# A weight's third part made by TensorE and ScalarE instead of VectorE, in a linear attention and gated FFN kernel

## The chip, the cores and the metric

The kernel runs on one core of one Trainium2 chip. The metric is the device time of one launch in microseconds, median of several runs. TensorE appears in the profile as PE (matmuls) and PEld (weight loads), VectorE as DVE, ScalarE as ACT, GpSimd as POOL, SyncE as SP. The kernel's transfers are issued by SyncE (SPq) and, fewer, by GpSimd (POOLq).

## What is computed

Two stages, in float32. The first is a recurrence with a decay per channel, over 768 steps, for 4 batches of 8 heads of 48 channels:

```
state = alpha[t][:, None] * state + outer(k[t], v[t])
y[t]  = q[t] @ state
```

The second takes y, laid out as x of 3072 tokens by 384, through a multiplicative FFN: `a = x @ w1; b = x @ w2; out = ((a * b) @ w3) @ w_out`, with w1 and w2 of 384x1024, w3 of 1024x1024 and w_out of 1024x384. The four weights arrive as 64-bit floats and must be turned into 32-bit ones on the chip.

## The kernel before

**The recurrence** is done in 24 chunks of 128 steps, six for each batch. For chunk n: `logs` takes the logarithm of alpha on ScalarE, `decays` sums it along time by a matmul with a triangle of ones (L271, and L274 from chunk 10) and takes two exponentials on ScalarE (L277, L278), `decayed` multiplies k and q by them on VectorE (L287), `transposed` turns them on TensorE and ScalarE copies them out of PSUM (L309, L311), `scores` multiplies q and k on TensorE and VectorE masks the product (L349, L352), `outer` forms the chunk's own state on TensorE (L321), and `attend_state` and `attend` add up y on TensorE (L369, L375), which ScalarE copies out (L379). The copies go to DRAM (xd, L246) and come back transposed three chunks at a time (xT, L391).

**The FFN's matmuls** run in fp32r, a float32 type that TensorE multiplies with a shortened mantissa. To reach float32's precision every operand is split in three parts h, l and m, and a product is made of h·h, l·l and m·m: `products` (L405) runs over the parts, and its callers weigh the sums. For w1 and w2, h is the value rounded and divided by P = 4096, l is what is left (w - P·h), and m is (P + 1)·h - w, which is h - l.

**Conversion.** `load_gates` fetches one unit of w1 or w2, 128x512 values as 64-bit words (raw, L189), and turns them into float32 by ScalarE (L197, L202) and VectorE (L198, L201, L204, L205, L207); then h by ScalarE (L214), l by VectorE (L216) and m by VectorE (L217). There are twelve units. The first six (half 0) hold the first 512 columns of both weights and are needed by the first gates; the other six (half 1) come later. `convert` advances these generators by a step at a time from the chunk loop.

**Order.** The loop over n (from line 583 on) calls, for each n: store, the loads of later chunks, attend_state(n - 1), scores(n), transposed(n + 1), a step of conversion, advance(n), attend(n - 1), outer(n), a piece of gate work, conversion, decayed(n + 2), logs(n + 4), decays(n + 3), conversion, gate work. From chunk 4 on x of three chunks is loaded (xT), split in its three parts by `split_x` (L397 on ScalarE, L398 and L399 on VectorE), and `gate` pieces (L405, L414, L416) fill TensorE between the chunks' own matmuls; the first such piece runs in chunk 7. A scheduler sets the order in which the instructions stand on each engine; every engine then works strictly in that order, and semaphores hold an instruction until its inputs are there and its buffer is free. PSUM is a ring of eight banks (`bank()`), taken in turn by all stages: eight in a chunk without gate work. Loads have three buffers for alpha and for k and q, five for v and four for raw words. After the chunks comes the rest of the gates, the folding of w3 and w_out into one, and the projection, almost all of it L405 on TensorE.

Of the kernel before, what the change touches and what calls it, by code (L numbers as in the profile page):

```python
# [10 lines left out]
FP32 = mybir.dt.float32  # L11
FP32R = mybir.dt.float32r
# [4 lines left out]
ALU = mybir.AluOpType  # L17
# [3 lines left out]
P = 4096.0  # L21
# [27 lines left out]
def kernel(  # L49
# [12 lines left out]
    nc = tc.nc  # L62
    B, H, S, D = q.shape
    C = 128
# [4 lines left out]
    NP = H // 2  # L69
# [12 lines left out]
    def pool(name, bufs, stack=ctx, **kw):  # L82
        return stack.enter_context(tc.tile_pool(name=name, bufs=bufs, **kw))
# [15 lines left out]
    p1 = pool("p1", 1, stack=part1, side="right", reuse_waits="tile")  # L99
    inp = pool("inp", 3, stack=part1, side="right", reuse_waits="tile")  # L100
    work = pool("work", 2, stack=part1, side="right", reuse_waits="tile")

    def bank():
        return ps.tile([C, 512], FP32, tag="bank", name="bank")
# [24 lines left out]
    def load_a(n):  # L129
        if n < N:  # L130
            st["a", n] = inp.tile([C, H, D], FP32, tag="ac", name="ac")
            nc.sync.dma_start(out=st["a", n], in_=rows(alpha, n))
# [8 lines left out]
    def load_v(n):  # L141
        if n < N:
            st["v", n] = vs[n % len(vs)]
            nc.sync.dma_start(out=st["v", n][:, :, 0:D], in_=rows(v, n))
# [10 lines left out]
    ident = const.tile([C, C], FP32, name="ident")  # L155
# [1 line left out]

    w12 = [p.tile([C, 3, 2, KM, CW], FP32R, name=f"w12{i}") for i, p in enumerate((w12ap, const))]

    utri = p1.tile([C, C], FP32, name="utri")  # L160
    after = p1.tile([C, C], FP32, name="after")

    sums = p1.tile([C, 2, C], FP32R, name="sums")
    keep = p1.tile([C, C], I32, name="keep")
    qks = [p1.tile([C, 2, H, DP], FP32, name=f"qk{i}") for i in range(3)]
    Ts = [p1.tile([C, NP, DP], FP32, name=f"T{i}") for i in range(2)]
# [11 lines left out]
    for x in qks:  # L178
        nc.vector.memset(x[:, :, :, D:], 0.0)
    make_identity(nc, ident)  # L180
    for x in Ts + decs:
        nc.gpsimd.memset(x, 0.0)

    def to_fp32(dst, *srcs):

        n, m = len(srcs) * srcs[0].shape[1], srcs[0].shape[1]
        raw = rawp.tile([C, n], I64, tag="raw", name="raw")
        for i, src in enumerate(srcs):
            nc.sync.dma_start(out=raw[:, ds(i * m, m)], in_=src)  # L189
        yield  # L190
        words = raw.bitcast(U32).rearrange("p (n w) -> p n w", w=2)
        low, high = words[:, :, 0], words[:, :, 1]

        mant = cvt.tile([C, n], FP32, tag="mant", name="mant")
        top = mant.bitcast(U32)
        rest = cvt.tile([C, n], FP32, tag="rest", name="rest", bufs=2)
        nc.scalar.activation(rest, low, AF.Copy, scale=2.0 ** -52)  # L197
        nc.vector.tensor_scalar(top, high, 0x000FFFFF, 0x00100000, op0=ALU.bitwise_and, op1=ALU.bitwise_or)  # L198

        power = cvt.tile([C, n], U32, tag="power", name="power", bufs=2)  # L200
        nc.vector.tensor_scalar(power, high, 20, 0x7FF, op0=ALU.logical_shift_right, op1=ALU.bitwise_and)  # L201
        nc.scalar.activation(power, power, AF.Relu, scale=2.0 ** 23, bias=rebias)  # L202
        yield
        nc.vector.scalar_tensor_tensor(mant, top, 2.0 ** -20, rest, op0=ALU.mult, op1=ALU.add)  # L204
        nc.vector.scalar_tensor_tensor(power, high, 0x80000000, power, op0=ALU.bitwise_and, op1=ALU.bitwise_or)  # L205
        to = mant if dst is None else dst()
        nc.vector.tensor_mul(to, mant, power.bitcast(FP32))  # L207
        yield
        return to

    def load_gates(i, kk, half):
        w = yield from to_fp32(None, (moe_w1, moe_w2)[i][ds(kk * C, C), ds(half * CW, CW)])
        h, l, m = (w12[half][:, x, i, kk, :] for x in range(3))
        nc.scalar.activation(h, w, AF.Copy, scale=(1.0 - 2.0 ** -13) / P)  # L214
        yield
        nc.vector.scalar_tensor_tensor(l, h.bitcast(FP32), -P, w, op0=ALU.mult, op1=ALU.add)  # L216
        nc.vector.scalar_tensor_tensor(m, h.bitcast(FP32), P + 1.0, w, op0=ALU.mult, op1=ALU.subtract)  # L217

    weights, begun = deque(), deque()

    def fetch(ahead=3):
        while weights and len(begun) < ahead:
# [19 lines left out]
    def store():  # L242

        while later:
            dst, src = later.popleft()
            nc.sync.dma_start(out=dst, in_=src)  # L246

    def last(n):
        return n % NCH == NCH - 1
# [15 lines left out]
    def decays(n):  # L265
        if n >= N:
            return
        lc = bank()[:, 0:DM]
        la = st.pop(("la", n))
        if n < LATE:  # L270
            nc.tensor.matmul(lc, utri if n % 2 else after, la, start=True, stop=True)  # L271
        else:
            for i in range(2):
                nc.tensor.matmul(lc, sums[:, n % 2], la[:, i], start=(i == 0), stop=(i == 1))  # L274

        e = st["e", n] = work.tile([C, 2, DM], FP32, tag="e", name="e", bufs=3)
        nc.scalar.activation(e[:, 0], lc, AF.Exp, scale=-1.0)  # L277
        mark["e", n] = nc.scalar.activation(e[:, 1], lc, AF.Exp).ins  # L278
        if n in ends:
            nc.gpsimd.dma_start(out=ends[n][0:1], in_=e[0:1, 0])  # L280
        if n + 1 in ends:
            nc.gpsimd.dma_start(out=ends[n + 1][1:2], in_=e[C - 1:C, 1])
        load_ends(n)
# [6 lines left out]
    def load_ends(n):  # L290
        if n not in ends:
            return
        with nc.allow_non_contiguous_dma(reason="single values to partitions"):
            for i in range(2):
                nc.gpsimd.dma_start(out=decs[n // 2 % 2][ds(DP * i, D)].rearrange("d m j -> d (m j)"),
                                    in_=ends[n].rearrange("m (j i d) -> i d (m j)", i=2, d=D)[i])
# [17 lines left out]
    def outer(n):  # L314
        if n >= N or last(n):
            return
        qk, vc = qks[n % 3], st["v", n]
        s1 = bank()[:, 0:NP * D].rearrange("p (j d) -> p j d", j=NP)
        for j in range(NP):
            for i in range(2):  # L320
                nc.tensor.matmul(s1[ds(DP * i, DP), j, :], qk[:, 0, 2 * j + i, :], vc[:, 2 * j + i, 0:D],  # L321
                                 start=True, stop=True)

        if n % 2:
            to = st["T", n] = work.tile([C, NP, D], FP32, tag="tmp", name="tmp")
        else:
            to = Ts[1][:, :, 0:D]
        if n % NCH == 0:
            nc.vector.tensor_copy(out=to, in_=s1)
        else:  # L330
            nc.vector.tensor_add(to, s1, Ts[n % 2][:, :, 0:D])
# [142 lines left out]
    def gate(g, f):  # L474
        yield from (late_gate if late else early_gate)(g, f)
# [73 lines left out]
    def run(pieces):  # L549

        for _ in range(pieces):
            if not fill:
                return
            try:
                next(fill[0])
            except StopIteration:
                fill.popleft()
# [5 lines left out]

    logs(0)
    decays(0)
    decayed(0)
    transposed(0)
# [15 lines left out]
    for n in range(N + 1):  # L583
        store()
        load_v(n + AHEAD - 1)
        load_a(n + 5)
        load_kq(n + AHEAD)
        if n:
            attend_state(n - 1)
        if n < N:  # L590
            scores(n)
        transposed(n + 1)
        if n - 2 in begin:
            g, tiles = begin[n - 2]
            split_x(g, 0)
            fill.extend(gate(g, f) for f in tiles)
        pieces = (0, 3, 3, 2)[(n - 6) % 4] if n > 5 else 0
        if n == 0:
            with after_marks(("qkT", 0)):
                logs(2)  # L600
            decays(2)
            with after_marks(("e", 2)):
                logs(3)
        early = n < 7
        behind = after_marks(("qkT", n + 1), ("qk", n + 1)) if early else ExitStack()
        if n < N - 2:
            with behind:
                convert(2 if n == 0 else 1, 2 if n == 0 else 3)
        advance(n)
        if n:  # L610
            attend(n - 1)
        outer(n)
        run(pieces > 0)
        if early:
            with after_marks(("qkT", n + 1), ("qk", n + 1)):
                convert(1)
        with after_marks(*[("ms", n)] * (n < 3)):
            decayed(n + 2)
        logs(n + 4)
        if n in begin:  # L620
            load_x(begin[n][0])
        convert(early and n > 2)
        run(pieces > 1)
        decays(n + 3)
        if n < N - 2:
            convert(early or n % 3 == 0)
        run(pieces > 2)
        if n == N - 3:
            while begun:
                convert(1)  # L630
            weights.extend(load_out(j) for j in range(KF))
            fetch(4)
# [91 lines left out]
```

## Time and profile before

| | us |
|---|---|
| median of five runs | 482.36 |
| the five runs | 484.13, 483.38, 482.36, 479.44, 479.32 |
| the profiled execution, its time | 484.13 |
| its span, first to last instruction | 482.4 |
| PE busy | 453.9 (94%) |
| DVE busy | 360.0 (75%) |
| ACT busy | 278.9 (58%) |
| POOL busy | 73.7 (15%) |
| mean granted clock of TensorE | 0.989 |

A span is counted from the first instruction's start to the last one's end; the execution's own time is 1.7 us longer. Busy times are averages over stages that are bound by different things, so the stage that a change touches must be looked at by itself. In the chain of waits every piece is the thing that the next piece waited for; "issue" is time for which the profile shows no wait. A transfer's issue is short, its landing some us later.

### The profile page before, as it was taken

To read this page: it belongs to the slowest core of one execution; us is meant where nothing else is said; L and a number is where in the kernel's file an instruction comes from. 1 tells how busy PE (TensorE), PEld (TensorE's weight loads), DVE (VectorE), ACT (ScalarE), POOL (GpSimd) and SP (SyncE) were. 2 spreads that over 40 slices of the span, in tenths; PEclk is the share of its full clock that TensorE was granted. 3 is DMA by queue.
4 is the path that set the end of the run, shared out by engine and by line. 5 is a ranking of instruction groups with operands and counts; after the bars stand their busy time and mean duration, and the time that the engine had idled before them with its cause. 6 is when DMAs were issued, how large, how long until landed. Compare 5 with 4: busy or idle time off the path is not lost.

```text
span 482.4 us, 9968 instructions
## 1 busy us (share of the span) xinstructions
PE 453.9 (94%) x3824; PEld 431.2 (89%) x3824; DVE 360.0 (75%) x582; ACT 278.9 (58%) x550; POOL 73.7 (15%) x138
## 2 busy tenths in 40 slices
PE   4788689999899999999999999999999999999996
PEld 2566479898798998999999999999999999999996
DVE  2779999986979666999999788846541966667761
ACT  4666667766667543899787576645553533333330
POOL 2221132112201300112232111111101100000000
PEclk9889999999899999999999999999999999999999
DMA  9999999899899974557775452122104865555511
GB/s 170 179 187 223 245 194 196 203 205 228 176 220 225 182 252 116 160 179 228 237 228 182 126 179 83 50 100 82 50 34 122 248 204 171 171 171 177 178 50 49
DMA packets 153583, 80.29 MB, mean 166 GB/s; under 512 B 104480, under 2 KB 145568, under 8 KB 153536
## 3 DMA queue, kind: packets, MB, share of 16 engines
q1 hardware_dynamic: 148016, 65.22, 55.4%
q0 software_dynamic: 5520, 14.43, 9.3%
q8 instruction: 30, 0.49, 0.4%
q14 instruction: 17, 0.14, 0.1%
HBM read 57.58 MB, written 22.06 MB: 165 GB/s over the span
## 4 chain that ended last, share of the span: by engine, by line
PE 81%; DVE 7%; DMA 5%; ACT 4%; issue 1%; SPq 1%; DVEq 0%; ACTq 0%
PE bank L405 68%; PE bank L375 3%; DMA ac<-in_alpha_dram 3%; PE bank L349 3%; PE bank L309 2%; DMA xd<-x 2%; PE bank L507 1%; DVE qk L287 1%; PE bank L369 1%; DMA raw<-in_moe_w_dram 1%; DVE ms L352 1%; PE bank L271 1%; PE bank L274 1%; PE bank L321 1%; DVE mant L207 1%
## 5 line engine op out<-in xcount | busy, mean ns | idle before, releaser
L405 PE MATMUL bank<-x,w 128*128 128x384 f32 x1152 | 211.4, 338 | 0.6 <-DVE ms L352 0.3
L405 PEld LDWEIGHTS bank<-x,w 128*128 128x128 f32 x1152 | 200.0, 188 | 2.6 <-issue 1.3
L405 PE MATMUL bank<-w3o,ab 128*128 128x384 f32 x576 | 100.2, 336 | 0.0
L405 PEld LDWEIGHTS bank<-w3o,ab 128*128 128x128 f32 x576 | 99.9, 188 | 0.0
L430 ACT ACTIVATE bank<-bank 128x384 f32<-128x384 f32 x98 | 46.8, 477 | 42.7 <-PE bank L405 42.4
L414 ACT ACTIVATE t<-bank 128x384 f32<-128x384 f32 x62 | 30.3, 493 | 59.3 <-PE bank L405 59.0
L480 POOL DMA_DIRECT2D abd<-ab x46 | 27.6, 599 | 132.2 <-DVE ab L466 124.5
L466 DVE TENSOR_TENSOR ab<-bank,r 128x384 f32<-128x384 f32 x45 | 24.9, 554 | 23.1 <-ACT bank L430 18.0
L536 DVE TENSOR_TENSOR ab<-abl,ab 128x1024 fp32r<-128x1024 f32 x24 | 29.4, 1225 | 13.5 <-ACT ab L535 13.5
L535 ACT ACTIVATE ab<-abl 128x1024 fp32r<-128x1024 f32 x24 | 25.5, 1062 | 21.3 <-PE bank L405 18.9
L405 PE MATMUL bank<-wo,w3T 128*128 128x384 f32 x192 | 35.9, 334 | 0.0
L349 PEld LDWEIGHTS bank<-qkT 48*128 48x128 f32 x384 | 25.5, 200 | 10.1 <-ACT qkT L311 3.7
L349 PE MATMUL bank<-qkT 48*128 48x128 f32 x384 | 30.3, 299 | 3.7 <-ACT qkT L311 2.4
L405 PEld LDWEIGHTS bank<-wo,w3T 128*128 128x128 f32 x192 | 33.5, 188 | 0.0
L352 DVE TENSOR_TENSOR ms<-bank,keep 128x512 int32<-128x512 int32 x48 | 31.2, 684 | 3.1 <-PE bank L349 3.1
L311 ACT COPY qkT<-bank 128x512 f32<-128x512 f32 x48 | 26.0, 586 | 12.6 <-PE bank L309 12.5
L416 DVE SCALAR_TENSOR_TENSOR o<-bank,t 128x384 f32<-128x384 f32 x24 | 13.4, 557 | 23.7 <-issue 15.2
L202 ACT ACTIVATE power<-power,rebias 128x512 uint32<-128x512 uint32 (+1 forms) x36 | 25.0, 698 | 9.5 <-DVE power L201 9.2
L197 ACT ACTIVATE rest<-raw 128x512 f32<-128x512 uint32 (+1 forms) x36 | 23.2, 648 | 12.2 <-DMA raw<-in_moe_w_dram 10.3
L287 DVE TENSOR_TENSOR qk<-kq,e 128x768 f32<-128x768 f32 x24 | 22.9, 953 | 10.0 <-ACT e L278 8.9
L537 DVE SCALAR_TENSOR_TENSOR ab<-ab,abl 128x1024 fp32r<-128x1024 f32 x24 | 29.2, 1218 | 0.0
L416 DVE SCALAR_TENSOR_TENSOR r<-bank,t 128x384 f32<-128x384 f32 x38 | 21.1, 554 | 10.6 <-ACT t L414 7.4
(75 smaller groups left out, 570.2 us busy)
## 6 DMA issues: line engine op xcount, KB each, us to landing
raw<-in_moe_w_dram SPq DMA_DIRECT2D x28, 512.0 KB, 5.3
abl<-abd SPq DMA_DIRECT2D x24, 512.0 KB, 4.6
abd<-ab POOLq DMA_DIRECT2D x46, 192.0 KB, 3.1
xT<-xd POOLq DMA_DIRECT2D x9, 576.0 KB, 4.5
ac<-in_alpha_dram SPq DMA_DIRECT2D x24, 192.0 KB, 5.5
kq<-in_k_dram SPq DMA_DIRECT2D x24, 192.0 KB, 5.5
kq<-in_q_dram SPq DMA_DIRECT2D x24, 192.0 KB, 4.4
v<-in_v_dram SPq DMA_DIRECT2D x24, 192.0 KB, 5.1
```

What stands on the lines that cost most here:

```text
L287: mark["qk", n] = nc.vector.tensor_mul(qks[n % 3][:, :, :, 0:D], st.pop(("kq", n)), st.pop(("e", n)).rearrange("p i (h d) -> p i h d", h=H ...
L311: mark["qkT", n] = nc.scalar.copy(qkT[:, :, :, ds(DP * half, DP)], tp[half]).ins
L349: nc.tensor.matmul(sc[i][:, j, :], qkT[r, 0, j, :], qkT[r, 1, j, :], start=True, stop=True)
L352: masked = nc.vector.tensor_tensor(ms[:, i].bitcast(I32), sc[i].bitcast(I32), keep_bc, op=ALU.bitwise_and)
L405: nc.tensor.matmul(p, w[part][i], x[part][i], start=start and part == parts[0] and i == 0, stop=stop and part == parts[-1] and i == n - 1, ...
L414: nc.scalar.activation(t, p1, AF.Copy, scale=(1.0 + 1.0 / P) * scale)
L416: nc.vector.scalar_tensor_tensor(to, p2, scale, t, op0=ALU.mult, op1=ALU.add)
L430: nc.scalar.activation(p, p, AF.Copy, scale=1.0 + 1.0 / P)
L480: (nc.gpsimd if late else nc.sync).dma_start(out=abd[g][:, f, :], in_=ab)
L535: nc.scalar.activation(t[:, 0], ab, AF.Copy, scale=1.0 - 2.0 ** -13)
L536: nc.vector.tensor_sub(t[:, 1], ab, t[:, 0].bitcast(FP32))
L537: nc.vector.scalar_tensor_tensor(t[:, 2], t[:, 0].bitcast(FP32), -1.0 - 1.0 / P, ab, op0=ALU.mult, op1=ALU.add)
```

## The change

For the six units of half 0, m isn't computed by VectorE any more. Two constant matrices are added, `signs`: the identity and the negative identity, in fp32r. `load_gates` puts (m, h, l) on a list, `thirds`. A new function, `third`, called once in each round of the chunk loop right after `outer(n)`, takes one entry, multiplies h by the identity and adds l times the negative identity in one PSUM bank (two matmuls of 512 columns), and ScalarE copies the bank to m. The units of half 1 keep the VectorE instruction.

The two float32 triangles `utri` and `after` lose their own place: they are made in a buffer of the pool from which the masks `ms` come, which has two, and `decays` reads the fp32r copies of them (`sums`) as float32 in the first ten chunks too. Their values are 0, 1 and -1 in either type.

```diff
-    utri = p1.tile([C, C], FP32, name="utri")
-    after = p1.tile([C, C], FP32, name="after")
+    made = work.tile([C, 2, NP, C], FP32, tag="ms", name="ms")
+    utri, after = made[:, 0, 0, :], made[:, 0, 1, :]
 
     sums = p1.tile([C, 2, C], FP32R, name="sums")
+    signs = p1.tile([C, 2, C], FP32R, name="signs")
...
     make_identity(nc, ident)
+    nc.gpsimd.tensor_copy(out=signs[:, 0], in_=ident)
+    nc.gpsimd.tensor_scalar_mul(signs[:, 1], ident, -1.0)
...
         nc.vector.scalar_tensor_tensor(l, h.bitcast(FP32), -P, w, op0=ALU.mult, op1=ALU.add)
-        nc.vector.scalar_tensor_tensor(m, h.bitcast(FP32), P + 1.0, w, op0=ALU.mult, op1=ALU.subtract)
-
-    weights, begun = deque(), deque()
+        if half:
+            nc.vector.scalar_tensor_tensor(m, h.bitcast(FP32), P + 1.0, w, op0=ALU.mult, op1=ALU.subtract)
+        else:
+            thirds.append((m, h, l))
+
+    weights, begun, thirds = deque(), deque(), deque()
+
+    def third():
+
+        if thirds:
+            m, h, l = thirds.popleft()
+            p = bank()
+            nc.tensor.matmul(p, signs[:, 0], h, start=True, stop=False)
+            nc.tensor.matmul(p, signs[:, 1], l, start=False, stop=True)
+            nc.scalar.copy(m, p)
...
         if n < LATE:
-            nc.tensor.matmul(lc, utri if n % 2 else after, la, start=True, stop=True)
+            nc.tensor.matmul(lc, sums[:, n % 2].bitcast(FP32), la, start=True, stop=True)
...
         outer(n)
+        third()
         run(pieces > 0)
```

## Prediction

> **What bounds the kernel now.** I read the page's slices first, to find the stage that the change touches, then the chain of waits inside it, then who fed that chain. The change lives between 20 and 64 us: the six units are converted there.
>
> The slices of the page: busy tenths per 12 us, granted TensorE clock, DMA share.
>
> ```profile
> PE   4788689999899999999999999999999999999996
> DVE  2779999986979666999999788846541966667761
> ACT  4666667766667543899787576645553533333330
> PEclk9889999999899999999999999999999999999999
> DMA  9999999899899974557775452122104865555511
> ```
>
> From slice 7 on PE has 9 but for one 8, and to the end of the span nothing else matters for long. In slices 4 to 6 VectorE has 9 and PE 6 to 8; DMA has 9 or 8 in all of the first fourteen. So the first 64 us have two candidates, VectorE and the DMA engines. The chain of waits names VectorE (start, us, what):
>
> ```profile
> 24.21 5.58 DMA raw<-in_moe_w_dram
> ...
> 35.44 0.60 DVE w L217
> ...
> 59.41 0.55 DVE w L217
> ...
> 60.96 1.20 DVE ms L352 x2
> 62.16 1.27 DVE x L398
> 63.43 1.28 DVE x L399
> ```
>
> The reader sees the first gate held by the split of x on VectorE (L398, L399), and L217, the line removed, on the chain. But the chain cannot tell an engine that is late from one that keeps pace with its input. SyncE's issue queue can (start, us):
>
> ```profile
> 46.67 0.85 SPq L139 DMA_DIRECT2D kq<-in_q_dram  x1
> 47.62 0.77 SPq L189 DMA_DIRECT2D raw<-in_moe_w_dram  x1
> 48.49 0.87 SPq L246 DMA_DIRECT2D xd<-x  x2
> 49.45 0.42 SPq L144 DMA_DIRECT2D v<-in_v_dram  x1
> 49.92 0.86 SPq L132 DMA_DIRECT2D ac<-in_alpha_dram  x1
> 50.88 2.75 SPq L138 DMA_DIRECT2D kq<-in_k_dram  x1
> 53.68 0.70 SPq L139 DMA_DIRECT2D kq<-in_q_dram  x1
> 54.48 0.64 SPq L391 DMA_DIRECT2D xT<-xd  x1
> ```
>
> Each issue starts within 0.1 us of the end of the one before, and so it goes from 4.6 to 77 us. I paired every transfer's completion record with the instruction that waits for it: they land one behind the other, about 1 us per 192 KB, and the compute engines' releases of buffers were all long past when SyncE issued. **Up to 77 us the transfers set their own pace** (DMA share 0.95 to 1.05 in the windows from 24 us), and VectorE trails each landing by little: the raw words of units 2 to 6 land at 29.79, 31.23, 38.95, 45.91, 53.22 and VectorE takes them at 29.82, 33.48, 41.48, 47.80, 54.35. xT(0) lands at 59.70. That is the wall: L398 can't start before ScalarE's part (59.72 + 1.16 = 60.9), against 62.16 now. Whatever VectorE saves, the first gate can gain **at most about 1.25 us** as long as the landings stay.
>
> **The change part by part.**
>
> *Removed:* six of
>
> ```profile
> L217 DVE SCALAR_TENSOR_TENSOR w<-w,mant 128x512 fp32r<-128x512 f32 x6 | 4.1, 684 | 0.0
> ```
>
> 4.1 us of busy time, 0.60 us each back to back, so 3.6 us of VectorE. Five lie after 30 us.
>
> *Added on ScalarE:* six copies bank to SBUF, 128x512. The nearest row is L311, same size and direction, 583 ns; bounds 376 (L379, 256 columns) and 715 (L202, 512 columns). I take 583: 3.5 us. ScalarE has 7.5 and 8.0 of 12 us in the two windows from 24 us, so room in the sum, but it works in order, below.
>
> *Added on PE:* twelve fp32r matmuls of 512 columns. No such row exists. Lower bound by L405, 384 columns: 120.72 us for 696 on the chain, 0.173 each; upper by L271, fp32, 0.91 us for two records, 0.455. By columns from L405: 0.173 x 512/384 = 0.231, nearest in type; 2.8 us, bounds 2.1 to 5.5. PE idles 2.4, 2.2 and 5.2 us in the windows 24:36, 36:48 and 48:64, which covers the sum; only unit 6's pair stands right before the first gate (0.46 us, counted below).
>
> *Set-up:* GpSimd makes signs, two operations of 128x128 (its L173 of that size: 0.28), ahead of the copy of the first triangle that decays(0) now reads. That copy ended at 3.09, would end at 3.65 to 3.7; decays(0) starts at 4.58 because alpha lands at 3.99. Cover 0.9 us, cost nothing. The triangles now stand in one of the two ms buffers; ms(1), the first to need it back, is written at 21.48, their last reader ends at 3.7. One bank more per chunk in a ring of eight makes some bank waits tighter: the wait for the unit's own copy, and outer, decays and transposes for a mask or copy just ahead.
>
> *Moved, and new waits.* SyncE's and GpSimd's later orders are the same in both programs. PE's isn't: third() puts each pair after outer(n) and before decays(n+3), so behind a pair that waits for its unit's h and l stand decays, attend_state, scores and transposes, and behind them ScalarE's exponentials. I carried this through by hand with the rows' durations:
>
> - Unit 2's pair stands after outer(2), which ended at 28.28. Its words land at 29.79, so h is done at about 34.0 and l at 35.6 (in the run before 34.46 and 35.44). PE waits some 5 us. decays(5) goes from 28.21 to 34.2, scores(3) from 32.12 to 36.2.
> - On ScalarE e(5) goes from 33.05 to 35.6, then the copy, then L197 of unit 4, which waits for its landing at 38.95 and now stands ahead of the qkT(4) copies: these go from 35.47 to 39.65, scores(4) from 38.17 to 41.0.
> - VectorE, without L217, isn't held as much: qk(5) 36.9 (38.62 before), ms(4) 44.1 (43.07), qk(6) 45.3 (45.73).
> - decays(8) 50.5 (50.28); transposes(7), behind the exponential of chunk 8, 55.6 (54.48); qk(8) 59.1 (60.01), ms(7) 60.3 (60.96); L399 ends at 64.1 instead of 64.8.
>
> So some 3 to 4 us are lost in chunks 3 and 4 and won back, because everything waits for landings there anyway; at the first gate **0.7 us ahead**.
>
> *Behind the first gate* the order is the same. PE is full from 72 to 96, so the lead is kept; then an alpha load and the xd stores end waits (5.96 and 7.34 us on the chain, at 103 and 117). These give it back unless the transfers move too. SyncE's first real wait is at 77.23: its issue of two stores takes 3.16 us, to ScalarE's copy of x, which moves with the lead. I keep 0.6 of the 0.7.
>
> *A rule that speaks against the change.* Granted clock: 0.86 in the window 24:36, and scores take
>
> ```profile
> 32.12 1.85 PE L349 MATMUL bank<-qkT 48*128 48x128 f32 x16 [2.40 <-ACT qkT L311]
> ...
> 44.60 1.16 PE L349 MATMUL bank<-qkT 48*128 48x128 f32 x16
> ```
>
> after a wait of 2.40 us and without one. The Trainium skill (TensorE: Matmul & The Clock Gate, What's actually happening) says that an idle window of about 3.4 us halves the clock. By it, a PE that waits 5 us for unit 2 stays at half clock one window longer, an estimate of 1.7 us more in chunk 3. By the row alone, each of scores, transposes and attend there costs 0.4 to 0.7 us more, about 1.6 us together. Either is absorbed in my carry, since transposes(7) wait for the exponential behind unit 6's landing, not for PE.
>
> **Sum.** Profiled execution: 484.13 us, span 482.4 and 1.7 around it; less 0.6 gives 483.5. It was the slowest of five runs; from their median, 482.36, the same step gives **481.8**.
>
> **Rivals.**
>
> 1. *VectorE was the bound.* For: the chain, and 11.3 of 12 us busy from 36 to 48. Against: the landings. Price: all six, 6 x 0.684 = 4.1 us: 478.3. Even that is under 1%.
> 2. *PE's wait for the conversions is not won back* (the other side). Place: the pair of unit 2, and 3 to 4, before decays. Price: scores(4) is late by 2.8 us in my carry, with the cold clock (1.6) and the largest matmul price (2.7 us more over twelve, 0.9 for the four issued by then) 5.3: 487.7. It decides from the point where chunk 7's masks end after 62.16, then every us goes through. For: ScalarE and PE become tied to each landing. Against: four chunks of slack follow.
> 3. *The gates shift against the transfers.* A lead frees SyncE's stores at 77 and 107 us earlier, and more than itself may drop out of the waits of 5.96 and 7.34: the two stores' issues take 2.67 and 2.00 us where such a one takes 0.38, so 2.3 and 1.6 us of waiting, with the 0.7 at most 4.6: 477.8. For: both waits end with the compute engines. Against: the landings behind them are one behind the other again within 4 us.
> 4. *It doesn't do what it says:* VectorE so far behind or PE so short of gaps that nothing moves: 482.4, beside my forecast.
>
> **How the numbers follow.** Forecast with rival 4: 0.62; rival 1: 0.15; rival 2: 0.18; rival 3: 0.05. A measurement of this kernel can tell about 1%, 4.8 us, from no change. Rival 1 ends within it; of rival 2 I give 0.13 to more than 4.8 us and 0.05 to less; and the far ends of rivals 1 and 3 lie so near the line that 0.07 falls beyond it. So faster 0.07, same 0.80, slower 0.13. Range: from all of rival 1, 478.3, to the whole price of rival 2, 487.7; rival 3's far end is left out.
>
> **What would show it.** Right: SyncE's issues as before up to 77 us; xT(0) landing at 59.5 to 60; VectorE with idle time before L198 of units 4 to 6, ended by the raw transfers; PE idle 4 to 6 us before unit 2's pair near 29 us, granted clock below 1 there; the first L405 group 0.3 to 1.3 us earlier. Wrong if the landings themselves move before 60 us, if L398 starts after 62.2, or if the lead changes sign between 100 and 125 us.

## The result, and the profile after

| | us |
|---|---|
| kernel before, median of 87 runs (478.34 to 486.62) | 481.66 |
| changed kernel, median of 45 runs (478.35 to 484.86) | 480.07 |
| ratio, 95% interval | 0.9973 [0.9961, 0.9985] |
| the changed kernel's profiled execution, its time and span | 480.0, 478.2 |

The change is worth 0.27%, some 1.3 us, less than the 1% that the prediction took for no change. The two profiled executions differ by three times as much, 482.4 against 478.2 us of span, so most of what these two traces show side by side is not the change. The table in the next section therefore has three profiles of each kernel.

The slices of the changed kernel (busy tenths of 12 us each, granted clock):

```profile
PE   4859999999999999999999999999999999999996
DVE  2767999997999566999998788745642876666761
PEclk9886999999999999999999999999999999999999
```

VectorE has 6 and 7 in the third and fourth slices (24 to 48 us) where it had 7 and 9: the relief is there, 7.30 and 8.64 us of 12 against 8.58 and 11.31. PE has 5 in the third slice where it had 8, then 9 up to the last slice, and its clock is at 8 and 6 tenths in the two. So another engine sets the pace of this stage: PE waits, and then works at a low clock. PE's timeline there (start, us, and in brackets the idle time ahead):

```profile
33.82 0.79 PE L232 MATMUL bank<-w,signs 128*128 128x512 f32 x1 [5.02 <-ACT w L217]
34.41 1.48 PE L286 MATMUL bank<-la,sums 128*128 128x384 f32 x2
35.83 1.11 PE L384 MATMUL bank<-qkT,T 48*64 48x128 f32 x10
36.87 0.79 PE L233 MATMUL bank<-w,signs 128*128 128x512 f32 x1
...
38.22 2.08 PE L364 MATMUL bank<-qkT 48*128 48x128 f32 x16
...
45.21 1.16 PE L364 MATMUL bank<-qkT 48*128 48x128 f32 x16
```

Unit 2's first matmul (L232) waits 5.02 us for h. The second (L233) starts 3 us later, because decays (L286) and ten of the sixteen matmuls of attend_state (L384) stand ahead of it in PE's order; l was there at 35.25. Scores(3) (L364, at 38.22) then takes 2.08 us, scores(4) (at 45.21) 1.16: the first at half clock, the second at full. The windows of the granted clock say how long: half from 33.43 to 43.67 us, 10.2 us.

The chain of waits of the changed kernel, which in the kernel before ran over L217 and the masks:

```profile
33.14 0.64 ACT w L217
33.82 0.79 PE bank L232
...
38.29 2.01 PE bank L364 x16
40.30 0.85 PE bank L324 x16
41.15 1.90 PE bank L390 x16
...
56.77 0.71 PE bank L324 x14
57.48 1.02 PE bank L390 x16
58.51 0.45 PE bank L336 x16
58.96 0.43 PE bank L232
59.39 0.23 PE bank L233
59.62 0.65 PE bank L286 x2
60.26 1.09 PE bank L364 x16
61.35 0.65 PE bank L324 x16
62.01 0.67 DVE ms L367
62.67 1.26 DVE x L413
63.94 1.27 DVE x L414
```

(Lines after the change are 15 higher from the chunk loop's helpers on: L413 and L414 are the split of x that was L398 and L399. ScalarE's L217 is the h that was L214; VectorE's L217 of the kernel before is gone for these units.) On this chain the split starts at 62.67, half a microsecond behind the 62.16 of before, though the transfer it needs, xT(0), lands at 59.48 against 59.70. ScalarE's part of the split is done at 62.23; VectorE comes to its own part only behind the masks of chunk 7 (L367), and these wait for the scores on PE. PE itself waits 0.88 us ahead of 56.77, for the exponential of chunk 8 (L293), and then has no gap up to the first gate (L420). One of the new pairs stands in the chain above, at 58.96, another right before the gate:

```profile
63.40 0.50 PE L232 MATMUL bank<-w,signs 128*128 128x512 f32 x1
63.74 0.39 PE L233 MATMUL bank<-w,signs 128*128 128x512 f32 x1
63.96 1.22 PE L420 MATMUL bank<-x,w 128*128 128x384 f32 x6
```

In the kernel before PE waits there for VectorE, which multiplies k and q (L287) right behind L217:

```profile
59.41 0.68 DVE L217 SCALAR_TENSOR_TENSOR w<-w,mant 128x512 fp32r<-128x512 f32 x1
60.01 0.95 DVE L287 TENSOR_TENSOR qk<-kq,e 128x768 f32<-128x768 f32 x1
...
61.11 0.71 PE L309 MATMUL bank<-ident,qk 64*128 64x64 f32 x16 [1.26 <-DVE qk L287]
...
63.23 1.32 PE L405 MATMUL bank<-x,w 128*128 128x384 f32 x6
```

The added work measured alone, by groups up to 70 us (count | busy us, mean ns of one | idle ahead):

```profile
L234 ACT CAST w<-bank 128x512 fp32r<-128x512 f32 x6 | 3.5, 584 | 1.4 <-PE bank L233 1.3
L232 PE MATMUL bank<-w,signs 128*128 128x512 f32 x6 | 3.3, 546 | 5.0 <-ACT w L217 5.0
L233 PE MATMUL bank<-w,signs 128*128 128x512 f32 x6 | 2.7, 456 | 0.0
```

SyncE's queue goes on as before, one issue behind the other: the load of k starts at 50.80 and takes 1.40 us, the load of q starts at 52.25, that of xT(0) at 53.16.

### The profile page after: what moved, and what is told of

It is laid out like the page before. It is cut to its first block, busy times and chain, and to the rows that moved or that the text cites. A ratio compares the mean times of both kernels' runs of the same rounds, so it can differ in the third digit from the quotient of the medians.

```text
span 478.2 us, 9993 instructions
## 1 busy us (share of the span) xinstructions
PE 458.0 (96%) x3836; PEld 434.9 (91%) x3836; DVE 356.7 (75%) x576; ACT 281.3 (59%) x556; POOL 72.0 (15%) x140
## 4 chain that ended last, share of the span: by engine, by line
PE 86%; DVE 6%; DMA 3%; ACT 2%; issue 1%; SPq 1%; DVEq 0%; ACTq 0%
PE bank L420 68%; PE bank L364 4%; PE bank L390 4%; PE bank L324 2%; PE bank L384 2%; PE bank L522 1%; DMA ac<-in_alpha_dram 1%; PE bank L286 1%; PE bank L336 1%; DMA raw<-in_moe_w_dram 1%; DVE ms L367 1%; PE bank L289 1%; DMA raw<-in_moe_w_out_dram 1%; DVE qk L302 1%; DVE x L413 1%
## 5 line engine op out<-in xcount | busy, mean ns | idle before, releaser
L420 PE MATMUL bank<-x,w 128*128 128x384 f32 x1152 | 211.4, 338 | 0.2 <-ACT x L394 0.2
L420 PEld LDWEIGHTS bank<-x,w 128*128 128x128 f32 x1152 | 200.4, 188 | 2.1 <-issue 0.7
L420 PE MATMUL bank<-w3o,ab 128*128 128x384 f32 x576 | 100.2, 336 | 0.0
L420 PEld LDWEIGHTS bank<-w3o,ab 128*128 128x128 f32 x576 | 99.9, 188 | 0.0
L429 ACT ACTIVATE t<-bank 128x384 f32<-128x384 f32 x62 | 30.5, 493 | 61.1 <-PE bank L420 60.9
L420 PE MATMUL bank<-wo,w3T 128*128 128x384 f32 x192 | 35.9, 334 | 0.0
L367 DVE TENSOR_TENSOR ms<-bank,keep 128x512 int32<-128x512 int32 x48 | 31.0, 683 | 6.0 <-PE bank L364 6.0
L420 PEld LDWEIGHTS bank<-wo,w3T 128*128 128x128 f32 x192 | 33.5, 188 | 0.0
L364 PEld LDWEIGHTS bank<-qkT 48*128 48x128 f32 x384 | 25.3, 200 | 7.4 <-issue 3.7
L364 PE MATMUL bank<-qkT 48*128 48x128 f32 x384 | 30.1, 300 | 1.3 <-DVE ms L367 1.3
L390 PE MATMUL bank<-ms,v 128*64 128x128 f32 x384 | 27.9, 291 | 0.0
```

Source lines behind the costliest of these rows:

```text
L364: nc.tensor.matmul(sc[i][:, j, :], qkT[r, 0, j, :], qkT[r, 1, j, :], start=True, stop=True)
L367: masked = nc.vector.tensor_tensor(ms[:, i].bitcast(I32), sc[i].bitcast(I32), keep_bc, op=ALU.bitwise_and)
L390: nc.tensor.matmul(to, vc[:, 2 * j + i, :], ms[:, i, j, :], start=(n % NCH == 0 and j % HP == 0), stop=(j % HP == HP - 1), skip_group_chec ...
L420: nc.tensor.matmul(p, w[part][i], x[part][i], start=start and part == parts[0] and i == 0, stop=stop and part == parts[-1] and i == n - 1, ...
L429: nc.scalar.activation(t, p1, AF.Copy, scale=(1.0 + 1.0 / P) * scale)
```

## The experiments

The forecast's theory is that the transfers set the pace to 77 us, so that VectorE's relief wins 1.25 us at most at the first gate. Its rivals are that VectorE was the bound (1), that PE's wait for the conversions costs (2), and that the gates shift against the transfers (3). After the first profiles two more questions stood: whether the waits at 100 to 125 us belong to the kernel (A) or to the execution (B), and, later, whether an exchange on ScalarE's queue is what the change brought (C).

Four landmarks carry all comparisons below: the landing of xT(0); the start of the first gate's first matmul (L405, or L420 after the change); the 23rd copy out of a gate's bank (L414, L429), at about 144 us; the end of the span. From the 25th such copy to the end each of the twelve profiles in the table has 323.24 to 323.34 us, so nothing of the difference lies behind about 155 us. "v issue" is SyncE's issue of the load of v right behind the stores that it reaches at about 77 us.

| kernel | xT(0) lands | first gate | behind the landing | v issue | 23rd copy | span |
|---|---|---|---|---|---|---|
| before, 1st profile | 59.70 | 63.23 | 3.53 | 80.48 | 148.39 | 482.35 |
| before, 2nd (b_again) | 59.90 | 62.65 | 2.75 | 80.33 | 143.88 | 479.46 |
| before, 3rd (b_rounds) | 58.80 | 61.66 | 2.86 | 80.32 | 144.14 | 478.14 |
| before, logarithm moved (b_log) | 58.58 | 61.25 | 2.67 | 79.02 | 143.93 | 477.96 |
| third part left out (e_no_third) | 59.40 | 63.45 | 4.05 | 80.15 | 144.34 | 478.31 |
| changed, 1st profile | 59.48 | 63.96 | 4.48 | 78.40 | 144.21 | 478.22 |
| changed, 2nd (a_again) | 58.49 | 62.59 | 4.10 | 76.81 | 142.79 | 476.75 |
| changed, 3rd (a_rounds) | 58.83 | 63.08 | 4.25 | 78.03 | 143.12 | 477.12 |
| changed, log and copy moved (a_log2) | 59.66 | 63.46 | 3.80 | 79.75 | 145.87 | 479.87 |
| added work alone (e_both) | 57.82 | 64.52 | 6.70 | 75.71 | 144.51 | 478.47 |
| pairs a round later (e_late) | 58.99 | 64.95 | 5.96 | 78.53 | 144.70 | 478.65 |
| the same, log and copy moved (e_late_log2) | 59.06 | 65.21 | 6.15 | 77.91 | 145.29 | 479.32 |

### Both kernels, profiled again

> The kernel before, unchanged, profiled a second time. In the two profiles at hand the waits at 100 to 125 us (alpha 5.96 us, xd stores 7.34 us) stand in the kernel before and not in the changed one, and the landings of the changed one run ahead more and more (0.2 us at 60 us, 2.2 at 80, 4.9 at 100, 5.8 at 117). Theory A, the waits belong to the kernel before: they are there again, 3 to 6 us of PE idle between 100 and 125 us, alpha landing near 109, span near 482. Theory B, the pace of the transfers differs from one execution to the next and the change has no part in it: landings after 60 us differ by over 1 us from the first profile, and the idle time at 100 to 125 us with them; span anywhere from 477 to 485.

> The changed kernel, profiled a second time. Theory A: PE busy over 24.5 of 25 us between 100 and 125 us again, alpha near 104, span near 478. Theory B: the landings after 60 us move by over 1 us, and PE idle time between 100 and 125 us may be back. Either way PE's wait of 5.0 us for unit 2's parts near 29 us and about 10 us of half clock behind it should be there again, since they come of the order of the instructions; the split of x for the first gate should again start at 62 to 63 us.

Spans 479.5 and 476.8. The kernel before has 26.00 of 26 us PE busy between 100 and 126 us this time, against 23.86 in the first profile, so the two big waits that stood between the first two profiles (alpha 5.96, xd 7.34) are not a property of the kernel before: Theory B, for these waits. It lost elsewhere: 1.52 us before scores at 148.66, then 3.4 us of half clock. What came back in the changed kernel is what the expectation named: PE waits 4.21 us for unit 2, and the clock is at half for 10.2 us, from 31.83 to 42.07.

### The relief alone, and the added work alone

```diff
-        nc.vector.scalar_tensor_tensor(m, h.bitcast(FP32), P + 1.0, w, ...)
+        if half:
+            nc.vector.scalar_tensor_tensor(m, h.bitcast(FP32), P + 1.0, w, ...)
...
-        return [([[w12[half][:, part, i, kk, ds(at, C)] ...
+        return [([[w12[half][:, part if half else part % 2, i, kk, ds(at, C)] ...
```

> The kernel before with the third part of the six units neither computed by VectorE nor by anything else; the products with half 0 read the first part in its place, so they are as many and as long, and the outputs of those columns are not the reference's. This is the relief of VectorE alone, without the added matmuls, copies and PE's wait. If the transfers set the pace up to 77 us (my forecast): the first gate gains 0.5 to 1.25 us, the split of x starts at 61 to 61.7 us, time 0.5 to 1.3 us below the kernel before, the same as the change within 0.6. If VectorE was the bound (rival 1): first gate 3.6 us or more earlier, time about 478. If the added matmuls and PE's wait cost something at the first gate (rival 2 in small), this kernel is faster than the changed one by that, 0.5 to 2 us.

480.75 us against 480.96 of the kernel before on the same chip, ratio 1.0004 [0.9974, 1.0034]. VectorE is busy for 356.5 us instead of 360.0, and no gain can be told: the interval goes from 1.3 us faster to 1.6 us slower, which leaves room for the 0.5 to 1.25 us of the forecast but not for the 4 us of rival 1. In the profile the first gate is at 63.45, and VectorE's split of x starts at 62.78, not at 61 to 61.7. The stretch from 48 to 60 us shows what came in its place:

```profile
48.00:60.00 12.00, 9.13 (x84) 7.11 (x84) 8.02 (x14) 6.54 (x14) 2.40 (x4) 0.57 0.94 236
```

(Columns: the stretch, its length, then busy time and count of PE, PEld, VectorE, ScalarE, GpSimd, the granted clock, the DMA share, GB/s.) No engine is full there, 8.02 of 12 us on VectorE; the clock is 0.57, after a wait of 3.28 us for a logarithm at 47.52. From 50.80 to the first gate PE has no gap of 0.1 us, until 59.95 at half clock. So in this profile the relief was turned into waiting and half clock on PE.

For the other half, the changed kernel gets L217 back and keeps the pairs, so that the third parts are written twice:

```diff
+        nc.vector.scalar_tensor_tensor(m, h.bitcast(FP32), P + 1.0, w, ...)
-        if half:
-            nc.vector.scalar_tensor_tensor(m, h.bitcast(FP32), P + 1.0, w, ...)
-        else:
+        if not half:
             thirds.append((m, h, l))
```

> The changed kernel with VectorE's instruction for the six third parts kept: VectorE writes them, and TensorE and ScalarE write them again. This is the price of what the change adds, without its relief. If everything added is hidden and the relief is the gain (my forecast): time as the kernel before, within 0.7 us. If PE's wait and the cold clock cost something at the first gate: 0.5 to 3 us slower than the kernel before. If the gain comes from the first gates' being shifted against the transfers whatever the direction: a time as that of the changed kernel, 1 to 2 us below the kernel before, with no idle PE at 100 to 125 us.

481.41 us, ratio 1.0011 [0.9983, 1.004]: as the kernel before. The first gate starts 6.70 us behind the landing of xT(0) instead of 2.7 to 3.5: PE waits 1.27 us for the multiplied k and q (L301), as in the kernel before, and has the two pairs besides. The landing itself is the earliest of all, 57.82, and the end is where the others end. So neither half of the change moves the time by anything that these intervals, 0.3% to either side, can tell.

### Fewer transfers

```diff
-        nc.sync.dma_start(out=st["kq", n][:, 0], in_=rows(k, n))
-        nc.sync.dma_start(out=st["kq", n][:, 1], in_=rows(q, n))
+        nc.sync.dma_start(out=st["kq", n], in_=rows(k, n))
...
-        ... st.pop(("kq", n)),
+        ... st.pop(("kq", n))[:, None].to_broadcast([C, 2, H, D]),
```

> The kernel before without the 24 transfers of q; k stands in q's place, so the outputs are not the reference's and everything else is the same. Nine of these transfers, 1 us each, land ahead of xT(0). If the transfers set the pace up to 77 us (my forecast): xT(0) lands 4 to 9 us earlier than 59.7 and the first gate's first copy out of the bank comes at 56 to 61 us instead of 64.0 to 64.6; time 3 to 8 us below the kernel before. If VectorE or the chain between the engines is as long by itself (rival 1): xT(0) may land earlier but the first gate stays at 63 to 64.6 us, and the time within 1 us of the kernel before.

> The changed kernel without the transfers of q, as the run beside it. With the transfers out of the way VectorE's relief should show. If VectorE is the next bound: 2 to 4 us faster than the other kernel without q. If PE's wait for the parts and the half clock behind it count once the transfers don't cover them (rival 2): as fast as the other or up to 4 us slower, with the first gate later than in the other.

487.86 (four runs) and 483.31 us (eight) against 479.51 of the kernel before on that chip; ratios 1.0185 [1.0145, 1.0225] and 1.0065 [1.0038, 1.0093]. Both are slower, which neither expectation had. Half of the forecast's wall shows: xT(0) lands 11.5 us earlier, at 48.24 and 47.89, more than the 4 to 9 us that were expected. The other half fails: ScalarE comes to the split 4.4 us behind the landing, at 52.59 and 52.25, and the first gate doesn't follow, 65.13 and 60.36. In the kernel without q and without the change, PE waits for VectorE:

```profile
55.92 1.16 PE L348 MATMUL bank<-qkT 48*128 48x128 f32 x16 [1.54 <-ACT qkT L310]
61.36 1.12 PE L308 MATMUL bank<-ident,qk 64*128 64x64 f32 x16 [4.27 <-DVE qk L286]
```

and VectorE has 12.00 of 12 us from 48 to 60. With the change that wait is gone, PE has 12.00 of 12 us there, and the kernel is 4.6 us faster than its twin. So in the kernel without q VectorE is a bound behind the transfers, and the change relieves it. Two reservations. The scheduler plans anew when transfers go, and the orders on VectorE, ScalarE, GpSimd and PE of these two kernels differ from those of the originals, so the 4.6 us is not a clean price of six instructions. And that both are slower than with q is more than their late or early gates: from the first gate to the 23rd copy they take 85.8 us, where the kernels of the table but the first take 79.8 to 82.7, with 3.2 and 5.5 us of PE idle and 10.0 and 3.4 us of half clock between 64 and 160 us. Of what their new order does there no run tells more.

### The pairs a round later

```diff
-        third()
+        while len(thirds) > 1 or thirds and n > 6:
+            third()
```

> The changed kernel with the pairs called one round of the chunk loop later (two in the round of chunk 7), so that PE finds h and l of the unit ready. If PE's wait of 4.2 to 5.0 us near 29 us and the 10.2 us of half clock behind it cost at the first gate: PE idle there falls under 2.5 us, scores(4) comes at 39 to 41 us instead of 45, the first gate's first copy comes 0.5 to 1.5 us earlier for the same landing of xT(0), and the time is 0.5 to 1.5 us below the changed kernel. If the landings alone count (my forecast's wall): time as the changed kernel within 0.5 us.

479.75 us, ratio 0.9993 [0.9967, 1.0018], beside 479.04 for the changed kernel on the same chip. PE finds unit 2's parts ready, and scores(4) comes at 39.87 instead of 45.21, as expected:

```profile
39.87 1.16 PE L364 MATMUL bank<-qkT 48*128 48x128 f32 x16
```

Five microseconds won in chunk 4, and the first gate is later than in the changed kernel: 64.95. Here the price sits at the other end. PE waits 1.64 us for a logarithm (L271), has no gap from 56.99 to the gate, works at half clock from 56.73 to 63.55, and two pairs (1.04 us) now stand right before the gate. None of what chunk 4 won is left at the first gate, as the forecast had it; how much these new costs covered, this run doesn't tell.

### The changed kernel once more, and the kernel before against itself

> The changed kernel again, beside the others on the same chip. In the two profiles of each kernel the time from 197 us to the end is the same within 0.1 us, and the first gate's first copy comes at 64.0 and 64.6 (before) and 63.9 and 65.2 (changed). If the change itself brings the 1.3 us of the medians: 479.4 to 480.2 against 480.9 to 481.7 of the kernel before on this chip. If the difference was of the chip or of chance: both medians within 0.6 us.

> The kernel before, once more, timed as the others are and with a third profile. Ratio to itself 1.000 within 0.002. The first gate's first matmul between 62.6 and 63.3 us as in its two profiles, PE's wait of 1.01 us near 67 again; the waits between 100 and 130 us there in some executions and not in others.

Changed: 479.04 us, ratio 0.9989 [0.9969, 1.0009]; median 479.51 of the kernel before. Here the change is worth 0.5 us, the interval holds no change, and by the expectation this is the case in which the 1.3 us were of the chip or of chance. The kernel before against itself: 479.77, ratio 0.9992 [0.9968, 1.0015]. With 12 runs a difference of 0.2% can't be told; that the change is a gain at all rests on the 45 and 87 runs of the result.

### The logarithm of chunk 10

In all profiles of the kernel before PE waits 1.01 us for the logarithm's fp32r copy in the first gate's round, in the changed kernel 0.46. The scheduler has put the logarithm (L256) ahead of a gate's copy there. That exchange, alone, made in the kernel before:

```diff
-        nc.scalar.activation(la, a, AF.Ln)
+        mark["la", n] = nc.scalar.activation(la, a, AF.Ln).ins
...
-            exact(r[-1], *factor, scale)
+            with after_marks(*[("la", LATE)] * ((g, f, len(r)) == (0, 0, 2))):
+                exact(r[-1], *factor, scale)
```

> The kernel before with one pair of ScalarE's instructions exchanged: the logarithm of chunk 10 stands ahead of the copy of the second product of the first gate (L414), as the scheduler happens to put it in the changed kernel; VectorE keeps its six instructions. Theory C: this exchange is what the change brought behind the first gate. PE's wait for the logarithm's copy near 67 us falls from 1.01 to 0.46 us, the time from the first gate's first matmul to the end falls from 414.8 or more (80.9 + 10.7 + 323.2) to 414.3, and the median comes 0.4 to 1.0 us under the kernel before. If the relief of VectorE or the later waits made the difference: the wait of 0.46 us may show, the time stays as the kernel before.

> The changed kernel with the logarithm's fp32r copy, too, ahead of that second copy (L429). Theory C: PE's wait near 67 us is gone (0.46 to 0), the time from the first gate's first matmul to the end falls from 414.0 to 414.3 to about 413.7, the median 0.3 to 0.6 us under the changed kernel. If the wait is taken up again a few us later (VectorE has 12 of 12 us from 72 to 84): no difference.

> The kernel with the pairs one round later, with the logarithm and its copy ahead of the first gate's second copy. If both steps add up: PE's wait of 1.02 us near 68 us is gone, the time from the first gate's first matmul to the end falls from 413.7 to about 412.7, the median 0.7 to 1.2 us under the kernel before. If later waits take it up: as the kernel before within 0.5 us.

The waits move as expected. The kernel before, then the same with the exchange:

```profile
66.62 0.45 PE L274 MATMUL bank<-la,sums 128*128 128x384 f32 x1 [1.01 <-ACT la L260]
```

```profile
65.64 0.45 PE L274 MATMUL bank<-la,sums 128*128 128x384 f32 x1 [0.46 <-ACT la L260]
```

With the copy moved too (a_log2, e_late_log2) the wait is gone. The times don't follow: 479.57, 479.57 and 479.95 us; ratios 0.9993 [0.9967, 1.0019], 0.9995 [0.9973, 1.0017] and 0.9987 [0.9963, 1.0011]. The intervals are too wide to exclude the 0.4 to 1.0 us that theory C asks for, but the landmarks speak against it: from the first gate to the end b_log has 416.7 us, a_log2 416.4 and e_late_log2 414.1, where C asks for 414.3, 413.7 and 412.7. In b_log the first gate is the earliest of all, 61.25, and the wait in it half a microsecond shorter; at the 23rd copy it has 143.93, as the others. The chain of b_log shows who took it:

```profile
84.16 6.87 DMA xd<-x
91.03 0.02 issue
91.05 0.02 ACTq L379
91.07 0.36 issue
91.43 0.47 ACT e L277
91.90 0.39 ACT e L278
92.29 0.04 issue
92.34 0.71 PE bank L309 x15
```

ScalarE's copy of x (L379) waits for the landing of an earlier store, from the buffer that it is to write (there are two of them), the exponentials stand behind it, and PE waits 1.51 us for them before its transposes (L309). No experiment beat both kernels.

## Why the prediction came out right, and where its steps were wrong

The range, the sign and "no change that can be told" hold. The forecast step is -0.6 us (481.8 against 482.36); measured is -1.3 with an interval from -0.7 to -1.9, and in the later runs (a_rounds) -0.5 with one from -1.5 to 0.4. The working behind it holds in part, and that the step came out with this sign is luck: the lead at the first gate from which it was taken isn't there.

**Removed.** Right in size: VectorE is busy for 3.95 us less from 24 to 48 us. Rival 1, that VectorE was the bound, falls with e_no_third: 3.5 us less work on it, ratio 1.0004. Rival 1 asked for 4.1 us.

**Added on ScalarE.** 584 ns a copy for 583 taken from L311.

**Added on PE.** The row from fewer columns was right for a matmul that follows its like: in e_late, where two pairs stand back to back, the third and fourth start 0.23 us behind the one ahead, as forecast (0.231). Not foreseen was the start of a pair: at full clock the second starts 0.34 us behind the first, so that a pair takes 0.56 us instead of 0.46. The records of L232 and L233 are longer than these steps, 546 and 456 ns in the mean, half-clock ones included.

**PE's wait for unit 2.** 5.02, 4.21 and 2.81 us in three profiles of the changed kernel; some 5 was carried. In the third the pair's turn comes at 30.05 instead of 28.80 us.

**The failing step is the end of the hand carry: "won back", "0.7 us ahead" at the first gate.** Carried and measured in the first profile: decays(5) 34.2 and 34.41, scores(3) 36.2 and 38.22, scores(4) 41.0 and 45.21, ms(4) 44.1 and 46.41, transposes(7) 55.6 and 56.77, end of the split 64.1 and 65.21. Two terms were wrong. The first is the clock: by the rule of the Trainium skill that was weighed (TensorE: Matmul & The Clock Gate, What's actually happening) it was to be one window more of half clock, 1.7 us. The trace has three in a row, 33.43 to 43.67, where the kernel before has one, 32.41 to 35.83; PE is busy for 10.18 of the 11 us from 33 to 44, with 0.53 of the clock, and sets the pace of that stretch, as the chain shows. The same section says that a busy window of about 3.4 us releases the clock; here a window without a gap, 36.84 to 40.26, did not. That most of this is absorbed was right: of the 4.2 us by which scores(4) is later than carried, 1.2 are left at transposes(7).

The second term is PE's own work behind transposes(7), and it wasn't absorbed. In the kernel before PE waits there for VectorE, 1.26 us; without L217 this wait is gone, but transposes(7) come later, at 56.77 instead of 54.49, released by the exponential of chunk 8, and from there PE has no gap until the first gate, 7.2 us, in which two pairs stand, 0.56 us each. The carry had allowed for the last pair alone, with 0.46. So PE's own order took the place of the wait. The split of x, which the prediction watched, doesn't hold the gate back: ScalarE's part starts 1.58, 1.21 and 1.49 us behind the landing in the changed kernel and 0.02 in the kernel before, but it is done 0.36 us before VectorE comes to x in all three profiles, and in e_late, where it starts 0.45 us behind the landing, the gate is later still. Measured from the landing, the first gate is later by 1.2 us in the mean of three profiles each (4.28 against 3.05), on the clock of the span by 0.7 (62.6 to 64.0 against 61.7 to 63.2). This is rival 2 with its sign and at most a quarter of its price of 5.3.

**The wall.** xT(0) landed at 58.5 to 59.5 in the changed kernel and 58.8 to 59.9 before: as forecast, the landings up to 60 us don't follow VectorE. ("Within 0.1 us" of each other SyncE's issues are but for one gap, 0.43 us at 63.01.) But the landing is not what the first gate waits for: in the kernel before VectorE comes to x 1.6 to 2.4 us behind it, and without q a landing 11.5 us earlier brought no earlier gate (65.13). And "set their own pace up to 77" stopped too early, and the pace isn't the same from one execution to the next: the 23rd copy stands at 142.8 to 145.9 in eleven of twelve profiles whether the first gate came at 61.25 or at 65.21. Between the two the transfers bind again in the kernel before, through the buffers of x (b_log's chain): in its three profiles and b_log the copy of chunk 9 starts 0.02 to 0.85 us behind the landing of the store that gives its buffer back, in the three of the changed kernel 2.0 to 3.3. This is why neither the 0.55 us of the logarithm nor an early gate was kept, and it corrects the line "PE is full from 72 to 96, so the lead is kept".

**The gain** is then not the one that was forecast. The first gate brings none, and the sign came by another road. Rival 3 had the right place, SyncE's stores at 77 us and the waits behind: in the seven kernels with pairs SyncE stands at 75.7 to 79.8 us there, mean 77.9, and in the five without at 79.0 to 80.5, mean 80.1; 0.9 of the 2.2 us is already there when xT(0) is issued. PE's idle time between 64 and 160 us goes with it: 1.7 to 2.0 us in the six profiles where SyncE stands before 79 us, 2.6 to 4.4 in the six where it stands later (a_log2, with 79.75, among them). For the changed kernel that is 1.85 us against 3.60 in the mean of three profiles each, more than the 0.7 us by which its gate is later. But rival 3 put it down to a lead of the gates, and there is none. Nor does SyncE wait for ScalarE at 77 us, as the prediction read the 2.67 us there: the copies that these stores send had ended at 71.91, and at 71.84 after the change. The earlier SyncE goes with the pairs, not with the relief: e_both has it (75.7) and e_no_third hasn't (80.15). And e_both's median is no lower for it; its first gate is the latest but two. A part of the 2.2 us lies in single issues of the loads of k, which take long though their buffer was given back 10 us earlier. The third profile of the kernel before, then the second of the changed one:

```profile
48.85 3.04 SPq L138 DMA_DIRECT2D kq<-in_k_dram  x1
51.94 1.51 SPq L139 DMA_DIRECT2D kq<-in_q_dram  x1
```

```profile
49.70 1.65 SPq L138 DMA_DIRECT2D kq<-in_k_dram  x1
51.39 0.80 SPq L139 DMA_DIRECT2D kq<-in_q_dram  x1
```

What holds these issues, and why the pairs would shorten them, was not tried, and so the cause of the gain stays open; five and seven profiles show that the two go together, and no more.

**What was to show it.** Right: SyncE's issues one behind the other; xT(0) between 59.5 and 60 in the first profile, by 0.02 us missed; PE's wait and the clock below 1. Wrong: the first L405 group 0.3 to 1.3 us earlier; L398 starting no later than 62.2, which had been named as the sign of an error; a lead that keeps its sign up to 125 us, since in the first profiles 0.7 us behind at the first gate became 4.2 ahead at the 23rd copy; and VectorE idle ahead of units 4 to 6. It takes the words of units 4 and 6, landed at 37.63 and 51.84, at 41.53 and 54.83 without idle time: it trails the landings as before, now behind masks that come late from PE.

## What to carry to other kernels

An instruction on the chain of waits is worth its time only up to the next bound: leave the work out once, as in e_no_third, before building its replacement on another engine. A replacement that ties two in-order engines to a third one's input pays at the place where it stands in their queues, here 0.7 to 1.2 us at the first gate, also where the wait that one sees first, 5 us in an earlier chunk, is mostly absorbed. And an engine that waits for the relieved one may have a queue of its own as long as the wait: follow its order up to the point that counts, with what the change adds to it. And where executions of one kernel differ by 4 us, two profiles side by side show mostly that; a handful of landmarks over several profiles tell what belongs to the change.

## What the runs showed of the hardware

- The granted clock stayed at half through a window in which PE had no gap. In the changed kernel's first profile the window 30.01 to 33.43 is idle; the next three, with 3.02, 3.42 and 3.41 us of PE busy time and 13, 27 and 44 records begun, are all at half clock, and only then does the full clock return. So a busy PE in the profile isn't enough to get the clock back; after waits of 5.02, 4.21 and (a_log2) 5.33 us ahead of unit 2 the half clock lasted 10.2 us each time, after 3.95 us (e_both) 6.8 us; after the 2.81 us of the third profile it did not come there at all, but for 6.8 us after a wait of 2.38 us at 51.30.
- Waits of 0.92 to 0.98 us ahead of scores near 150 were not followed by a window of half clock; one of 1.52 us was (b_again, 151.21 to 154.62), but waits of 1.28 to 1.65 us there in four other profiles were not. So the length of a wait alone doesn't decide it.
- SyncE takes 1.4 to 3.5 us for every load of k that it issues between 48 and 77 us, 48 in the twelve profiles, where its twin of the same size, the load of q behind it, takes 0.64 to 0.83 in 26 of 48, though k's buffer was given back 9.5 us earlier or more. In b_log the DMA engines' share fell to 0.16 from 53.15 to 54.05 us, behind such an issue (49.13 to 51.32) and a long one for q (1.96 us); so these engines can run dry while SyncE is never without an issue.
